# Transposing softmax weights on VectorE in squares of 32x32, with transfers inside SBUF, instead of on TensorE

## The chip, the cores and the metric

The kernel runs on one core of a Trainium2 chip. A core has five engines that run beside one another, each through a queue of its own in order: TensorE (PE in the profile; its weight loads are PEld), VectorE (DVE), ScalarE (ACT), GpSimd (POOL) and SyncE (SP), which here issues every transfer. The metric is the device time of one execution in microseconds, lower is better.

## The reference

Pooled attention, whose output goes through an expert layer with a rational activation:

```python
def _attn_ref(q, k, v):                      # q, k, v: (8, 8, 576, 64) float32
    k_p = k.reshape(B, H, Sp, pool, D).mean(axis=3)      # pool = 8, Sp = 72
    v_p = v.reshape(B, H, Sp, pool, D).mean(axis=3)
    scores = scale * np.matmul(q, k_p.transpose(0, 1, 3, 2))
    scores = scores - np.max(scores, axis=-1, keepdims=True)
    attn = np.exp(scores)
    attn = attn / (np.sum(attn, axis=-1, keepdims=True) + 1e-09)
    return np.matmul(attn, v_p)

def _moe_ref(x, w_in, w_out, a, b):          # x: (4608, 512), w_in: (512, 2048)
    h = x @ w_in
    P = a[0] + a[1] * h + a[2] * h * h + a[3] * h * h * h
    Q = 1.0 + np.abs(b[0]) * np.abs(h) + np.abs(b[1]) * h * h
    return (P / (Q + 1e-06)) @ w_out
```

## The kernel before

The 4608 tokens go through in 18 blocks of 256 tokens (`TOK`), a block being two tiles of 128. For each block `attend` computes the attention's output x, transposed (features on the partitions) and split into a high and a low part; then eight units of 256 hidden features each follow: `mm1` (TensorE, bank ph), `rational` (ScalarE, VectorE, GpSimd; result gh and gl) and `mm2` (TensorE, bank po). Matrix products run in fp32r on such split operands, so each is made of three products, and those of the weighted values of four. Blocks 0 to 3 are interleaved in a special order while the weights are loaded; blocks 4 to 17 run one after the other, eight units each.

The attention of one tile t (`attention`, lines 563 to 616) goes like this. q is loaded (qt, two buffers). TensorE transposes it per pair of heads (pq), ScalarE copies that to SBUF (qT, a single buffer). TensorE multiplies it with the pooled keys kpT (ps, two halves). VectorE takes the maximum (mx) and subtracts it (e), ScalarE exponentiates, VectorE sums (sm) and inverts, GpSimd multiplies: e now holds the softmax weights, 128 tokens x 8 heads x 72 keys. Two heads are 144 columns; the last 128 of them are the main part, the first 16 the rest. The main part is transposed by TensorE into a PSUM bank (pm, lines 607 to 609), ScalarE rounds it into the high part hi, VectorE subtracts to get the low part lo (the two tiles am, one buffer each, lines 610 to 612). The rest goes through er, pr and ar. When both tiles of a block are done, `values` multiplies the weights with the pooled values (pv) and splits the result into x.

The order of all of it is written out by a planner (`Plan`, lines 100 to 241), which runs when the kernel is built. Every operation is registered with its engine, an assumed cost, its buffers and its dependences. `solve` first gives every operation a due time, going back from its users: the user's due time less `slack` (1.6, in `attend` 2.5) times the cost plus 0.25 us (line 152). It then simulates the engines: it takes again and again the operation that can start first, and among those that can start at the same time the one due first. Buffers of a ring go to tiles in order, except in the rings called loose. A tile that an operation only `claims` is taken with it, too: the pq transposes claim qT. For transfers it assumes the issue cost (0.45 us), the bytes at 360 GB/s on one shared bus, another 1.9 us to land, and at most eight in flight (lines 213 to 216). `issue` writes the instructions out in that order, so each engine's order is fixed; on the chip, semaphores hold an instruction until its operands are there. Since all instructions are recorded in line 240, the profile tells them apart by their tiles.

PSUM's eight banks are four ps_o (po, and the rational's rp), two ps_h (ph) and two ps_a (all of the attention's banks).

Of the kernel before, what the change touches and what calls it, by code (L numbers as in the profile page):

```python
# [8 lines left out]
F32 = mybir.dt.float32  # L9
# [3 lines left out]
ALU = mybir.AluOpType  # L13
# [86 lines left out]
class Plan:  # L100
# [47 lines left out]
    def solve(self):  # L148
        for op in reversed(self.ops):
            for d in op.deps:  # L150
                d.users.append(op)
                d.due = min(d.due, op.due - d.slack * (d.cost + 0.25))
        for op in self.ops:
            op.wait, op.ready = len(op.deps), max(0.0, op.due - op.early)
        engs = {}
        for op in self.ops:
            engs.setdefault(op.eng, [])
            if not op.wait:
                engs[op.eng].append(op)
        at = dict.fromkeys(engs, 0.0)  # L160
        port = bus = 0.0
        flights = [0.0] * 8
        done, order = 0, []
        while done < len(self.ops):
            best = None
            for e, cands in engs.items():
                pick = None
                opts = []
                for op in cands:
                    t = max(at[e], op.ready)  # L170
                    if op.port:
                        t = max(t, port)
                    if op.bytes:
                        t = max(t, flights[0])
                    need = {}
                    for b in op.bufs:
                        if not b.held:
                            r = b.ring
                            n = need.setdefault(id(r), [r, 0])
                            if not r.loose and b not in r.queue[:len(op.bufs)]:  # L180
                                break
                            n[1] += 1
                    else:
                        for r, n in need.values():
                            mine = [b for b in op.bufs if not b.held and b.ring is r]
                            if len(r.free) < n or not r.loose and any(
                                    b not in mine for b in r.queue[:n]):
                                break
                            t = max(t, sorted(r.free)[n - 1])
                        else:  # L190
                            opts.append((t, op))
                if not opts:
                    continue
                t0 = min(t for t, _ in opts)
                t, op = min(((t, op) for t, op in opts if t <= t0 + 0.02),
                            key=lambda x: (x[1].due, x[1].seq))
                if best is None or t < best[0]:
                    best = t, op
            assert best, "the plan is stuck at " + ", ".join(
                str([b.name for b in op.bufs]) for c in engs.values() for op in c[:3])  # L200
            t, op = best
            engs[op.eng].remove(op)
            for b in op.bufs:
                if not b.held:
                    b.held = True
                    r = b.ring
                    r.free.remove(min(r.free))
                    r.queue.remove(b)
            op.start, op.end = t, t + op.cost
            at[op.eng] = op.end  # L210
            if op.port:
                port = op.end
            if op.bytes:
                bus = max(bus, op.end) + op.bytes / 360e3
                op.end = bus + 1.9
                flights = sorted(flights[1:] + [op.end])
            for b in op.bufs:
                b.left -= 1
                b.it = max(b.it or 0.0, op.end)
                if not b.left:  # L220
                    b.ring.free.append(b.it)
            for u in op.users:
                u.wait -= 1
                u.ready = max(u.ready, op.end + (self.LAT if u.eng != op.eng else 0.0))
                if not u.wait:
                    engs[u.eng].append(u)
            order.append(op)
            done += 1
        self.order = order
# [29 lines left out]
def tile_pooled_attention_then_rational_moe(  # L259
# [20 lines left out]
    P = 128  # L280
    G = 8
    SP = S // G
    NJ = H // 2
    REM = 2 * SP - P
    RW = G * D
    TOK = 256
# [29 lines left out]
    def bank(where, name, shape):  # L316
        return new(where, where, shape, F32, name)
# [236 lines left out]
    def segs(t0, n):  # L554
# [5 lines left out]
            t = e  # L560
        return r

    def attention(t, am, ar):

        sg = segs(t * P, P)
        col = slice((t % 2) * P, (t % 2 + 1) * P)
        qt = new("work2", "qt", [P, H, D], F32, f"qt{t}")
        for r0, r1, n in sg:
            s0 = t * P + r0 - n * S
            dma(512, qt[r0:r1], q[n, :, s0:s0 + (r1 - r0), :].rearrange("h s d -> s h d"))  # L570
        pq = bank("ps_a", f"pq{t}", [P, NJ, P])
        qT = new("work1", "qT", [P, NJ * P], F32, f"qT{t}").rearrange("p (j t) -> p j t", j=NJ)
        pe(109 * NJ, [
            ("transpose", (pq[:, j, :],
                           qt[:, 2 * j:2 * j + 2, :].rearrange("s h d -> s (h d)"), ident), {})
            for j in range(NJ)], claims=(qT,))
        act(NJ * P).copy(qT, pq)
        e = new("work2", "e", [P, H, SP], F32, f"e{t}")
        mx = new("work2", "mx", [P, H], F32, f"mx{t}")
        sm = new("work2", "sm", [P, H], F32, f"sm{t}")  # L580
        for c in range(2):
            hs = slice(4 * c, 4 * c + 4)
            ps = bank("ps_a", f"ps{t}_{c}", [P, 4, SP])
            pe(245 * 2 * len(sg), [
                mm(ps[r0:r1, 2 * jj:2 * jj + 2, :], qT[:, 2 * c + jj, r0:r1],
                   kpT[n % 2][:, 2 * c + jj, :], True, True)
                for jj in range(2) for r0, r1, n in sg], claims=(e, mx, sm))
            dve(4 * SP).tensor_reduce(out=mx[:, hs], in_=ps, op=ALU.max, axis=AX.X)
            dve(4 * SP).tensor_tensor(
                out=e[:, hs, :], in0=ps,  # L590
                in1=mx[:, hs].unsqueeze(2).to_broadcast([P, 4, SP]), op=ALU.subtract)
        act(H * SP).activation(e, e, AF.Exp, scale=D ** -0.5)
        dve(H * SP).tensor_reduce(out=sm, in_=e, op=ALU.add, axis=AX.X)
        dve(0).tensor_scalar(out=sm, in0=sm, scalar1=1e-9, scalar2=None, op0=ALU.add)
        dve(40).reciprocal(sm, sm)
        gp(400).tensor_tensor(
            out=e, in0=e, in1=sm.unsqueeze(2).to_broadcast([P, H, SP]), op=ALU.mult)
        ef = e.rearrange("p (j h) s -> p j (h s)", h=2)
        er = new("work2", "er", [P, 2, 2, 2, 2, REM], F32R, f"er{t}")
        rem = ef[:, :, 0:REM].rearrange("p (c m) r -> p c m r", m=2)  # L600
        for c in range(2):
            esrc = rem[:, c].unsqueeze(1).to_broadcast([P, 2, 2, REM])
            act(90).copy(er[:, c, 0], esrc)
            dve(60, port=True).tensor_tensor(
                out=er[:, c, 1], in0=esrc, in1=er[:, c, 0].bitcast(F32), op=ALU.subtract)
        hi, lo = am
        pm = bank("ps_a", f"pm{t}", [P, NJ, P])
        pe(109 * NJ, [("transpose", (pm[:, j, :], ef[:, j, REM:], ident), {})
                      for j in range(NJ)], claims=am)
        act(NJ * P).copy(hi[:, :, col], pm)  # L610
        dve(NJ * P).tensor_tensor(
            out=lo[:, :, col], in0=pm, in1=hi[:, :, col].bitcast(F32), op=ALU.subtract)
        pr = new("ps_a", "ps_a", [P, 2, P], F32R, f"pr{t}")
        pe(63 * 2, [("transpose", (pr[:, c, :], er[:, c].rearrange("p a g m r -> p (a g m r)"),
                                   identr), {}) for c in range(2)], claims=(ar,))
        act(2 * P).copy(ar[:, :, col], pr.bitcast(F32))
# [28 lines left out]
    def attend(i):  # L645

        for _, _, n in segs(i * TOK, TOK):
            if n not in prepared:
                prepared.add(n)
                prep_k(n)  # L650
                (prep_v_early if n < 2 else prep_v)(n)
        am = [new("work1", f"am{s}", [P, NJ, TOK], F32R, f"am{s}_{i}") for s in range(2)]
        ar = new("work1", "ar", [P, 2, TOK], F32R, f"ar{i}")
        for m in range(2):
            attention(2 * i + m, am, ar)
        return values(i, am, ar)


# [171 lines left out]
```

## Time and profile before

| | us |
|---|---|
| median of 3 executions | 998.79 |
| their range | 996.03 to 999.13 |
| the profiled execution | 996.57 |
| its span, first to last instruction | 994.6 |

| engine | busy us | share of the span | instructions |
|---|---|---|---|
| TensorE matmuls | 968.0 | 97% | 6396 |
| TensorE weight loads | 871.4 | 88% | 6396 |
| VectorE | 743.8 | 75% | 1299 |
| ScalarE | 710.6 | 71% | 1216 |
| GpSimd | 507.1 | 51% | 443 |

Transfers move 64.26 MB, at 65 GB/s in the mean. A row of the groups reads: line, engine, operation, written tile <- read tiles, shapes, count | busy time in us, mean ns of one | idle time of the engine before them, and what ended it. In the timeline a row is start, duration, engine, operation; xN are N instructions merged, and a bracket gives the idle time ahead.

### The profile page before, as it was taken

The page shows a single profiled execution, that of the slowest core. Times are in us where ns is not written, and L with a number is a line of the kernel's source. Part 1 is how long each engine was busy: PE and PEld are TensorE (multiplying, and loading weights), DVE is VectorE, ACT ScalarE, POOL GpSimd, SP SyncE. Part 2 cuts the span into 40 slices and gives each one's busy share as a digit, 9 for nine tenths or more (in the row PEclk, how much of TensorE's full clock was granted, in tenths as well). Part 3 has the DMA queues.
Part 4 walks back from the last instruction along what each step waited for, and adds up shares of the span by engine and source line. Part 5 has one row for each costly group of instructions (what it writes and reads, how often), then busy time and mean ns, then how long its engine had stood idle before and what let it go on. Part 6 is the DMA issues. An engine that isn't in the chain of part 4 may idle for free.

```text
span 994.6 us, 16951 instructions
## 1 busy us (share of the span) xinstructions
PE 968.0 (97%) x6396; PEld 871.4 (88%) x6396; DVE 743.8 (75%) x1299; ACT 710.6 (71%) x1216; POOL 507.1 (51%) x443
## 2 busy tenths in 40 slices
PE   7898999999999999999999999999999999999997
PEld 6787898889898899899899989898989898999996
DVE  4798977888687867687778687787778686767664
ACT  3578888878666766777777776687767776777764
POOL 4355666757444734353654464454643473445343
PEclk9699999999999999999999999999999999999999
DMA  9946020233111302010401031002201020100000
GB/s 301 332 148 257 22 86 1 70 106 128 32 33 25 88 1 86 1 43 7 128 22 43 6 107 44 21 27 61 89 11 39 20 87 1 44 1 22 1 22 21
DMA packets 62705, 64.26 MB, mean 65 GB/s; under 512 B 39968, under 2 KB 39968, under 8 KB 62624
## 3 DMA queue, kind: packets, MB, share of 16 engines
q1 hardware_dynamic: 62624, 63.19, 20.6%
q8 instruction: 50, 0.82, 0.4%
q14 instruction: 31, 0.25, 0.1%
HBM read 50.60 MB, written 12.58 MB: 64 GB/s over the span
## 4 chain that ended last, share of the span: by engine, by line
PE 91%; DVE 4%; ACT 2%; issue 2%; POOL 1%; POOLq 0%; ACTq 0%; DVEq 0%
PE ph L240 40%; PE po L240 38%; PE pv L240 4%; PE ps L240 4%; PE pm L240 2%; PE pq L240 1%; DVE t L240 1%; PE pvs L240 1%; PE warm L240 1%; PE pr L240 1%; POOL w L240 0%; PE pk L240 0%; DVE rp L240 0%; DVE m_win L240 0%; DVE m_wout L240 0%
## 5 line engine op out<-in xcount | busy, mean ns | idle before, releaser
L240 PEld LDWEIGHTS ph<-x,win 128*128 128x128 f32 x3264 | 474.0, 189 | 63.0 <-issue 7.5
L240 PE MATMUL ph<-x,win 128*128 128x256 f32 x3264 | 502.3, 283 | 3.0 <-DVE t L240 0.5
L240 PE MATMUL po<-wout,gh 128*128 128x512 f32 x1152 | 354.5, 397 | 1.4 <-ACT gh L240 1.4
L240 POOL TENSOR_TENSOR w<-w,r 128x512 f32<-128x512 f32 x144 | 189.7, 1318 | 258.0 <-ACT r L240 252.9
L240 POOL TENSOR_TENSOR gl<-t,gh 128x512 fp32r<-128x512 f32 x144 | 190.5, 1323 | 154.7 <-ACT gh L240 106.0
L240 PEld LDWEIGHTS po<-wout,gh 128*128 128x128 f32 x1152 | 183.6, 189 | 12.1 <-ACT gh L240 2.3
L240 PE MATMUL po<-wout,gl 128*128 128x512 f32 x576 | 183.0, 399 | 0.3 <-POOL gl L240 0.2
L240 DVE TENSOR_TENSOR t<-t,ph 128x512 f32<-128x512 f32 x144 | 98.5, 684 | 101.3 <-ACT t L240 97.1
L240 DVE SCALAR_TENSOR_TENSOR t<-t,abn,rp 128x512 f32<-128x512 f32 x144 | 107.2, 745 | 71.9 <-ACT rp L240 70.7
L240 ACT ACTIVATE rp<-w,cbias 128x512 f32<-128x512 f32 x144 | 99.4, 690 | 41.6 <-POOL w L240 34.8
L240 ACT ACTIVATE t<-ph,abn 128x512 f32<-128x512 f32 x144 | 109.3, 769 | 20.6 <-PE ph L240 20.0
L240 ACT ACTIVATE r<-w,abn 128x512 f32<-128x512 f32 x144 | 117.6, 816 | 7.0 <-POOL gl L240 0.7
L240 ACT ACTIVATE w<-ph 128x512 f32<-128x512 f32 x144 | 85.9, 596 | 47.3 <-PE ph L240 44.3
L240 ACT CAST gh<-t 128x512 fp32r<-128x512 f32 x144 | 88.1, 612 | 43.2 <-DVE t L240 42.9
L240 DVE SCALAR_TENSOR_TENSOR t<-t,abn,ph 128x512 f32<-128x512 f32 x144 | 107.5, 747 | 5.0 <-ACT w L240 0.7
L240 DVE SCALAR_TENSOR_TENSOR t<-rp,t 128x512 f32<-128x512 f32 x144 | 99.1, 688 | 3.8
L240 DVE SCALAR_TENSOR_TENSOR rp<-w,rp 128x512 f32<-128x512 f32 x144 | 99.2, 689 | 0.2
L240 PEld LDWEIGHTS po<-wout,gl 128*128 128x128 f32 x576 | 91.4, 189 | 5.1 <-POOL gl L240 1.1
L240 ACT ACTIVATE rp<-rp 128x512 f32<-128x512 f32 x144 | 83.8, 582 | 3.8
L240 ACT COPY qT<-pq 128x512 f32<-128x512 f32 x36 | 21.1, 585 | 48.5 <-PE pq L240 47.3
L240 POOL TENSOR_TENSOR e<-e,sm 128x576 f32<-128x576 f32 x36 | 41.0, 1153 | 28.5 <-DVE sm L240 21.5
L240 PE MATMUL ps<-kpT,qT 128*128 128x144 f32 (+1 forms) x320 | 45.6, 298 | 3.8 <-DVE e L240 2.5
(88 smaller groups left out, 896.9 us busy)
## 6 DMA issues: line engine op xcount, KB each, us to landing
out_dram<-ob SPq DMA_DIRECT2D x18, 512.0 KB, 2.9
qt<-in_q_dram SPq DMA_DIRECT2D x32, 256.0 KB, 3.1
rwin<-in_moe_w_in_dram SPq DMA_DIRECT2D x8, 1024.0 KB, 7.7
rwout<-in_moe_w_out_dram SPq DMA_DIRECT2D x8, 1024.0 KB, 11.5
st_k<-in_k_dram SPq DMA_DIRECT2D x12, 512.0 KB, 4.4
st_v<-in_v_dram SPq DMA_DIRECT2D x12, 512.0 KB, 3.8
st_v<-in_v_dram SPq DMA_DIRECT2D x48, 64.0 KB, 3.6
early<-in_k_dram SPq DMA_DIRECT2D x4, 512.0 KB, 7.2
```

The costliest lines, as they stand in the source:

```text
L240: getattr(engines[op.eng], name)(*map(value, args), **{k: value(v) for k, v in kw.items()})
```

## The change

Blocks 0 to 3 (tiles 0 to 7) stay as they are. For tiles 8 to 35 the four transposes pm, their copy and subtraction are left out. VectorE transposes the main part of e in squares of 32x32 into a tile es, which is taken from the ring of qT; within a square rows and columns are exchanged, but the squares stay where they were. Sixteen transfers on SP's queue then bring the squares of partition group a and column group g, for all four pairs of heads, to partition group g and column group a of lo, as plain fp32. The planner is told 48 KB for each of them (they carry 32 x 4 x 32 x 4 bytes, 16 KB). When both tiles of the block are there, one ScalarE cast over 128x1024 makes hi, and one VectorE subtraction over as many elements, in place, makes lo. In the planner, the due time of whatever a transfer's user needs goes back by another 5 us times the slack, for all transfers of the kernel.

```diff
-                d.due = min(d.due, op.due - d.slack * (d.cost + 0.25))
+                d.due = min(d.due, op.due - d.slack * (d.cost + 0.25 + (5.0 if d.bytes else 0.0)))
...
+    HB = 32
+
...
         hi, lo = am
-        pm = bank("ps_a", f"pm{t}", [P, NJ, P])
-        pe(109 * NJ, [("transpose", (pm[:, j, :], ef[:, j, REM:], ident), {})
-                      for j in range(NJ)], claims=am)
-        act(NJ * P).copy(hi[:, :, col], pm)
-        dve(NJ * P).tensor_tensor(
-            out=lo[:, :, col], in0=pm, in1=hi[:, :, col].bitcast(F32), op=ALU.subtract)
+        if t >= 8:
+
+            es = new("work1", "qT", [P, NJ * P], F32, f"es{t}").rearrange(
+                "p (j g s) -> p j g s", j=NJ, s=HB)
+            dve(NJ * P).transpose(es, ef[:, :, REM:].rearrange("p j (g s) -> p j g s", s=HB))
+            for a in range(4):
+                for g in range(4):
+                    s0 = (t % 2) * P + a * HB
+                    dma(48, lo[g * HB:(g + 1) * HB, :, s0:s0 + HB].bitcast(F32),
+                        es[a * HB:(a + 1) * HB, :, g, :])
+        else:
+            pm = bank("ps_a", f"pm{t}", [P, NJ, P])
+            pe(109 * NJ, [("transpose", (pm[:, j, :], ef[:, j, REM:], ident), {})
+                          for j in range(NJ)], claims=am)
+            act(NJ * P).copy(hi[:, :, col], pm)
+            dve(NJ * P).tensor_tensor(
+                out=lo[:, :, col], in0=pm, in1=hi[:, :, col].bitcast(F32), op=ALU.subtract)
...
         for m in range(2):
             attention(2 * i + m, am, ar)
+        if i >= 4:
+            hi, lo = (x.rearrange("p j t -> p (j t)") for x in am)
+            act(NJ * TOK).copy(hi, lo.bitcast(F32))
+            dve(NJ * TOK, port=True).tensor_tensor(
+                out=lo, in0=lo.bitcast(F32), in1=hi.bitcast(F32), op=ALU.subtract)
         return values(i, am, ar)
```

## The prediction

> **What bounds the kernel now.** I read the page first: the busy shares and the chain that ended last.
>
> ```profile
> span 994.6 us, 16951 instructions
> PE 968.0 (97%) x6396; PEld 871.4 (88%) x6396; DVE 743.8 (75%) x1299; ACT 710.6 (71%) x1216; POOL 507.1 (51%) x443
> ...
> PE 91%; DVE 4%; ACT 2%; issue 2%; POOL 1%; POOLq 0%; ACTq 0%; DVEq 0%
> ```
>
> TensorE is busy 97% of the span and makes up 91% of the chain; VectorE and ScalarE have a quarter of their time free. Next the table by stretches (the columns after the stretch are its length, then busy time of PE, PEld, DVE, ACT and POOL, the granted clock, the share of the DMA engines and GB/s), and TensorE's waits from 250 to 960 us.
>
> ```profile
> 0.00:25.00 25.00, 17.79 (x109) 15.57 (x109) 11.53 (x34) 8.43 (x18) 11.29 (x51) 0.96 1.03 302
> 25.00:50.00 25.00, 20.49 (x113) 18.47 (x114) 18.36 (x36) 14.37 (x28) 8.83 (x5) 0.63 1.02 329
> 50.00:950.00 900.00, 890.54 (x5952) 803.99 (x5951) 689.98 (x1198) 663.05 (x1135) 470.36 (x375) 1.00 0.17 53
> ```
>
> ```profile
> PE pq L240 <- PE ps L240: 0.6, 1, 0.6
> PE pl L240 <- ACT kpT L240: 0.3, 1, 0.3
> PE pl L240 <- DVE ks L240: 0.2, 1, 0.2
> ```
>
> Only the first 50 us are bound by loads (DMA share above 1, clock down to 0.63). Over the 900 us behind them TensorE is idle for 9.5 us, and over 710 of them it waits for another engine just 1.1 us in all. So the stage that the change touches, blocks 4 to 17, is TensorE's own work in a row: work taken from TensorE comes off the time one for one, and any new wait in its queue goes on in the same way.
>
> **Removed.** Of each of the tiles 8 to 35 (28 of 36): four TensorE transposes, a ScalarE copy, a VectorE subtraction.
>
> ```profile
> 550.82 0.87 PE pm L240 x8
> ```
>
> ```profile
> L240 PE MATMUL pm<-identr,e 128*128 128x128 f32 x144 | 20.0, 278 | 2.0 <-DVE t L240 0.9 <-ACT qT L240 0.8 <-DVE vr L240 0.4
> L240 DVE TENSOR_TENSOR am<-pm,am 128x512 fp32r<-128x512 f32 x36 | 23.6, 686 | 4.7 <-ACT am L240 4.4
> L240 ACT CAST am<-pm 128x512 fp32r<-128x512 f32 x36 | 19.8, 587 | 7.1 <-PE pm L240 6.8
> ```
>
> The piece of the chain holds both tiles of a block: eight transposes in 0.87 us, 0.109 us each. The 278 ns of the group row is one matmul's own length, which overlaps its neighbours; the queue moves on by 0.109. Fourteen blocks times 0.87 is **12.2 us** off TensorE. The Trainium skill (TensorE: Matmul & The Clock Gate, Part 4: PE-mode transpose) gives about 275 ns for a transpose in one kernel's context; the trace's 278 agrees, but priced by it the removal would be an estimated 31 us, and the chain's 0.109 decides against that. The freed PSUM bank I cost at nothing: the 1.1 us of waits above hold no wait for one that is worth more.
>
> **Added on the compute engines.** VectorE gets 28 transposes of 128x512 (no such row), and per block one subtraction of 128x1024 out of SBUF; ScalarE one cast of 128x1024 per block.
>
> ```profile
> L240 ACT CAST win<-m_win 128x1024 fp32r<-128x1024 f32 x8 | 8.4, 1045 | 0.0
> L240 DVE SCALAR_TENSOR_TENSOR m_win<-rwin,m_win 128x1024 int32<-128x1024 int32 x8 | 10.2, 1276 | 0.0
> L240 DVE TENSOR_SCALAR m_win<-m_win 128x1024 int32<-128x1024 int32 x8 | 7.5, 932 | 0.0
> L240 DVE TENSOR_TENSOR st_k<-st_k 128x512 f32<-128x512 f32 x12 | 10.1, 857 | 0.0
> ```
>
> A transpose lies between 0.47 us (half of the 932 ns) and 0.86 (the two-input row of 512); I take 0.69, what the removed subtraction took for as many elements. VectorE then has 2 x 0.69 + 1.28 - 2 x 0.69 = 1.3 us more per block (0.8 to 1.6), ScalarE 1.045 - 2 x 0.587 = 0.13 less. Both hide behind TensorE: with 18 us more, VectorE is at about 79% of the 900. If that cover were gone, the 18 us would be lost.
>
> **Added on SP's queue.** Sixteen transfers per tile of 16 KB, 448 in all, each 128 pieces of 128 bytes. No transfer inside SBUF is in the trace; the nearest rows are the trains of 64 KB loads of v and the loads of q.
>
> ```profile
> 480.36 1.73 SPq L240 DMA_DIRECT2D st_v<-in_v_dram  x4
> ```
>
> ```profile
> L240 SPq DMA_DIRECT2D st_v<-in_v_dram x6: 329/417/424, 480.4 to 483.0; - x6
> DMA to landing us min/median/max: 2.1/2.2/4.2
> ```
>
> ```profile
> 636.00:641.00 5.00, 5.00 (x35) 4.55 (x34) 3.48 (x5) 3.31 (x6) 3.12 (x3) 1.00 0.23 52
> ```
>
> ```profile
> 580.41 1.26 SPq L240 DMA_DIRECT2D st_v<-in_v_dram  x3
> 583.27 0.38 SPq L240 DMA_DIRECT2D st_v<-in_v_dram  x1
> ```
>
> ```profile
> SPq L240 <- PE pq L240: 373.5, 25, 41.3
> SPq L240 <- DMA st_v<-in_v_dram: 9.5, 4, 3.0
> ```
>
> Four issues take 1.73 us, 0.43 each; I take 0.45 (single ones go from 0.33 to 0.42), landing 2.1 us after its issue when nothing large is in the way. The stretch at 636 us holds one load of q, 256 KB in 1024 pieces of 256 bytes: 0.23 x 5.0 x 16 engines / 1024 = 18 ns a piece. At that price a transfer holds its engines for 128 / 16 x 18 ns = 0.14 us, well under the 0.45 of its issue, so issue sets the pace. A train of sixteen lasts 15 x 0.45 + 2.1 = 8.9 us: 7.1 at 0.33, and about 12 with the landings of 5 us that the loads behind 583 us show. The plan that fixes the order counts 0.45 for each issue, 48 KB at 360 GB/s and 1.9 us to land: 16 x 0.45 + 0.14 + 1.9 = 9.2. Plan and rows agree within 0.3 us, and that is the main reason for my forecast. SP spends 448 x 0.45 = 202 us on it, out of a queue that by the row above has 373 us of waiting for pq alone; loads of q and stores of out queue behind a train, and both have time.
>
> The Trainium skill (DMA: Bandwidth & Descriptors, Specifications) speaks against such pieces: transfers under 512 bytes are read, modified and written back. By it a piece could cost an estimated 36 ns rather than 18, or 0.29 us a transfer; no run here shows it, and it is still below the issue's 0.45, so the sum is the same by both, and only the ring's chance below grows.
>
> **The new waits.** The squares lie in the single buffer that qT has. So ScalarE's copy qT of the next tile must wait until the sixteen transfers have landed, and behind it in ScalarE's queue stand the activations of the expert stage, while TensorE's ps matmuls, in order, wait for that copy. Second, the cast and the subtraction of a block follow the second train, and TensorE's pv waits for both. Third, lo has one buffer: the first train of a block waits for pv of the block before. Before, both tiles of a block overlapped (one pm piece for two tiles); now they run one behind the other.
>
> ```profile
> 531.16 0.58 ACT L240 COPY qT<-pq 128x512 f32<-128x512 f32 x1
> 540.92 1.15 POOL L240 TENSOR_TENSOR e<-e,sm 128x576 f32<-128x576 f32 x1 [5.79 <-DVE sm L240]
> ...
> 636.35 0.59 ACT L240 COPY qT<-pq 128x512 f32<-128x512 f32 x1
> 651.92 2.26 POOL L240 TENSOR_TENSOR e<-e,sm 128x576 f32<-128x576 f32 x2
> ```
>
> ```profile
> 245.43 0.34 PE L240 MATMUL pv<-am,vm 128*128 128x128 f32 x2
> ...
> 924.72 0.40 PE L240 MATMUL pv<-am,vm 128*128 128x256 f32 x2
> ```
>
> From qT to the end of the normalised weights: 542.07 - 531.16 = 10.9 us when it presses, 653.07 - 636.35 = 16.7 when it doesn't. With 0.7 for the transpose and 8.9 for the train a tile holds the ring 20.5 us, two tiles 41. From the pv of block 4 to that of block 17 (13 blocks) a block lasts 52.25 us, 51.4 after the change. So the ring fits with 10 us to spare.
>
> What is left is the order on TensorE: a train later than planned holds ps or pv back. The plan puts the pq transposes behind the landing (they claim qT), the chip doesn't need that: 0.44 + 0.07 us; and half a piece of waiting for ScalarE (0.35) and for TensorE (0.24). That is about 1.1 us of give at each of 28 joints. Six blocks also load k and v; there SP stands at a transfer that hasn't landed from 581.67 to 583.27, 1.6 us. Once in each of these blocks: 6 x (1.6 - 1.1) = 3.0 us. Bounds: nothing, and case B below.
>
> **The head.** The planner now counts 5 us more behind every transfer, times a slack of 1.6 (weights) or 2.5 (q, k, v): those become due 4.5 us earlier against the weights, and loads of the first 50 us can change places. One 512 KB load ahead of a needed one costs 512 KB / 329 GB/s = 1.6 us, the reverse gains as much; two of them bound this at -3 and +3. I take 0.
>
> **Sum.** 996.57 (the profiled execution, 2.0 more than its span) - 12.2 + 3.0 + 0 = 987.4. That execution is 2.2 us under the median 998.79; on the scale of the median: **989.6 us**.
>
> **Rivals.**
>
> - B, trains land late (slower). One mechanism: transfers share their landing with other traffic and SP stops at outstanding ones, so each train takes 2 us longer than planned. Price 28 x (2.0 - 1.1) = 25 us: 989.6 - 3.0 + 25 = 1012. It decides from 28 x (d - 1.1) = 12.2, d = 1.5 us. For it: landings of up to 5 us and the 9.5 us of SP's waits. Against: those are four waits beside 512 KB loads; most trains have none.
> - C, the ring binds (slower). If a tile takes the slow 16.7 us, two need 2 x (16.7 + 0.7 + 8.9) = 52.6 against 51.4: 1.2 x 14 = 17 us, 1007. With pieces three times as dear it becomes worse, since the engines' 0.43 us then meets the issue. Against: the 16.7 us tile was one that nobody waited for.
> - D, the gain is eaten: trains late by 1.5 us, or the head worse by 3 and the joints by 6: 998.
> - E, no joint costs anything and the head gains 3: 998.8 - 12.2 - 3 = 983.6.
>
> **How the numbers follow.** A, the forecast, 0.52; E 0.10; D 0.13; B 0.17; C 0.08. What a measurement can tell is 0.3%, 3 us. Faster (under 995.8): A and E, 0.62. Same: D, 0.13. Slower: B and C, 0.25. A's own range is 985 to 995; the range from 982 to 1010 takes in E, D, most of C and the milder half of B.
>
> **What would show it.** Right: pm gone from the chain after block 4, TensorE's busy time 12 us down over the stretch from 50 us on, its waits there still a few us, trains of about 9 us, VectorE up by some 18 us. Wrong: rows with ps waiting for qT, or pv for am, of tens of us in TensorE's waits (B), qT copies waiting for transfers at every tile and a distance of pv to pv above 52 us (C), or first 100 us that differ by more than 3 us in TensorE's busy time (the head).

## The result: 1032.0 us, 3.4% slower

The changed kernel's median is 1031.99 us; the kernel before, timed beside it, had 997.7. The ratio is 1.0341 with a 95% interval of 1.032 to 1.0363. The forecast was 989.6, with 1010 as the upper end.

From the page of the changed kernel: span, busy times, and the chain that ended last by engine and by line.

```profile
span 1029.1 us, 17440 instructions
PE 972.3 (94%) x6284; PEld 870.4 (85%) x6284; DVE 759.9 (74%) x1313; ACT 706.8 (69%) x1202; POOL 504.9 (49%) x443
...
PE 41%; SPq 20%; DVE 11%; ACT 9%; DMA 6%; issue 6%; POOL 5%; POOLq 0%; ACTq 0%; DVEq 0%
SPq L240 20%; PE ph L240 17%; PE po L240 14%; PE pv L240 4%; DVE t L240 4%; DMA am<-es 4%; PE ps L240 3%; POOL e L240 2%; POOL w L240 1%; POOL gl L240 1%; DVE am L240 1%; ACT r L240 1%; DVE sm L240 1%; ACT rp L240 1%; ACT t L240 1%
```

TensorE has 112 instructions fewer and yet 4 us more of busy time. It makes up 41% of the chain instead of 91%; 20% is now SP's queue issuing transfers, which had no part in the chain before. The span is 34.5 us longer: 4.3 of it busy time of TensorE, 30.2 idle time (56.8 against 26.6 us).

The waits of TensorE from 250 to 990 us, and ScalarE's waits for the transfers, over the whole span:

```profile
PE ps L240 <- ACT qT L240: 13.6, 12, 2.1
PE pv L240 <- DVE am L240: 5.6, 10, 0.8
PE pv L240 <- ACT am L240: 5.2, 8, 1.1
PE pv L240 <- ACT qT L240: 2.1, 2, 1.5
PE pv L240 <- ACT kpT L240: 0.8, 1, 0.8
PE pv L240 <- DMA qt<-in_q_dram: 0.8, 2, 0.6
```

```profile
ACT am L240 <- DMA am<-es: 32.4, 13, 3.5
...
ACT qT L240 <- DMA am<-es: 16.4, 10, 3.8
```

These are the two joints that the prediction named: ps behind qT, pv behind am. Both hang on the trains of sixteen transfers. Here they are, as issues and as one train of the timeline:

```profile
L240 SPq DMA_DIRECT2D am<-es x448: 585/599/1607, 206.6 to 960.9; - x150
DMA to landing us min/median/max: 1.8/1.8/5.2
```

```profile
513.88 10.25 SPq L240 DMA_DIRECT2D am<-es  x16
...
544.58 11.30 SPq L240 DMA_DIRECT2D am<-es  x16
```

An issue takes 0.60 us, not 0.45, and with the gap behind it one follows the other every (10.25 - 0.60) / 15 = 0.643 us. The landing is quick, 1.8 us in the median. The first of the two trains lasts 10.25 - 0.60 + 1.8 = 11.4 us, where the plan counts 9.2: 2.2 us late. The second takes a microsecond more, so 2.2 us is the lateness of a train that nothing disturbs. There are 28 joints; at 23 of them (13 and 10 in the rows above) ScalarE waits for the landing.

The new work on the compute engines costs what it was thought to:

```profile
L240 DVE STREAM_TRANSPOSE es<-e 128x512 f32<-128x512 f32 x28 | 19.9, 710 | 6.6 <-POOL e L240 5.7
L240 DVE TENSOR_TENSOR am<-am,am 128x1024 fp32r<-128x1024 f32 x14 | 17.1, 1224 | 31.8 <-ACT am L240 25.7 <-DMA st_k<-in_k_dram 6.1
L240 ACT CAST am<-am 128x1024 fp32r<-128x1024 f32 x14 | 14.7, 1047 | 32.4 <-DMA am<-es 32.4
```

The waits by name add up to less than the loss, and the busy time went up. The timeline and the stretches around one late pv show a reason (columns as in the prediction: length, busy times of PE, PEld, DVE, ACT and POOL, then the granted clock):

```profile
629.55 0.63 PE L240 MATMUL po<-wout,gl 128*128 128x512 f32 x2
631.31 0.41 PE L240 MATMUL pv<-am,vm 128*128 128x64 f32 x2 [1.13 <-ACT am L240]
...
632.57 0.58 PE L240 MATMUL pv<-am,vm 128*128 128x64 f32 x3 [0.79 <-DVE am L240]
...
637.81 1.11 PE L240 MATMUL ph<-x,win 128*128 128x256 f32 x4
```

```profile
628.00:632.00 4.00, 2.65 (x17) 1.96 (x15) 0.71 (x1) 1.76 (x3) 0.16 (x1) 1.00 0.08 12
632.00:636.00 4.00, 3.43 (x20) 3.43 (x21) 3.59 (x6) 3.48 (x6) 1.28 (x1) 0.65 0.01 4
636.00:640.00 4.00, 4.00 (x19) 3.81 (x18) 2.25 (x5) 1.74 (x4) 1.27 (x1) 0.50 0.00 0
640.00:644.00 4.00, 4.00 (x30) 3.75 (x30) 3.96 (x7) 0.94 (x2) 1.56 (x1) 1.00 0.00 0
```

TensorE stands 1.13 us before pv and 0.79 us in the middle of it, and then works at half clock for the greater part of two stretches. By the granted clock that is (1 - 0.65) x 4 + (1 - 0.50) x 4 = 3.4 us of work lost behind 1.9 us of waiting. The Trainium skill (TensorE: Matmul & The Clock Gate, Part 1: The HAM clock gate) says that an idle window of about 3.4 us brings the half clock. Here no single wait came near that: two short ones with a few matmuls between them were followed by it. One place can't show where the limit lies.

### The profile page after: what moved, and what is told of

It reads as the page before. It is cut to its first block, busy times and chain, and to the rows that moved or that the text cites. A ratio compares the mean times of both kernels' runs of the same rounds, so it can differ in the third digit from the quotient of the medians.

```text
span 1029.1 us, 17440 instructions
## 1 busy us (share of the span) xinstructions
PE 972.3 (94%) x6284; PEld 870.4 (85%) x6284; DVE 759.9 (74%) x1313; ACT 706.8 (69%) x1202; POOL 504.9 (49%) x443
## 4 chain that ended last, share of the span: by engine, by line
PE 41%; SPq 20%; DVE 11%; ACT 9%; DMA 6%; issue 6%; POOL 5%; POOLq 0%; ACTq 0%; DVEq 0%
SPq L240 20%; PE ph L240 17%; PE po L240 14%; PE pv L240 4%; DVE t L240 4%; DMA am<-es 4%; PE ps L240 3%; POOL e L240 2%; POOL w L240 1%; POOL gl L240 1%; DVE am L240 1%; ACT r L240 1%; DVE sm L240 1%; ACT rp L240 1%; ACT t L240 1%
## 5 line engine op out<-in xcount | busy, mean ns | idle before, releaser
L240 PE MATMUL po<-wout,gh 128*128 128x512 f32 x1152 | 358.8, 401 | 2.2 <-ACT gh L240 1.4
L240 PEld LDWEIGHTS po<-wout,gh 128*128 128x128 f32 x1152 | 187.3, 191 | 15.6 <-ACT gh L240 2.5
L240 PEld LDWEIGHTS po<-wout,gl 128*128 128x128 f32 x576 | 93.6, 190 | 8.4 <-POOL gl L240 2.2
L240 PE MATMUL pv<-am,vm 128*128 128x256 f32 (+3 forms) x288 | 54.5, 308 | 16.5 <-DVE am L240 6.1
L240 PEld LDWEIGHTS pv<-am,vm 128*128 128x128 f32 x288 | 46.8, 212 | 24.3 <-DVE am L240 9.7
L240 PE MATMUL ps<-kpT,qT 128*128 128x144 f32 (+1 forms) x320 | 46.5, 302 | 18.4 <-ACT qT L240 15.2
```

The costliest lines, as they stand in the source:

```text
L240: getattr(engines[op.eng], name)(*map(value, args), **{k: value(v) for k, v in kw.items()})
```

## The experiments

All but e4, which starts from the kernel before, start from the changed kernel. Theory **M**: the trains last longer on the chip than in the plan, so the fixed order puts the waiting instructions too early. Rival **R**: two tiles in a row over one buffer are too long for a block, whatever the plan counts. Rival **K**: the transfers or VectorE's transposes slow other work. Rival **H**: the edit of the due times costs the time. The kernel before was timed beside each, at 996 to 999 us.

**e1: the plan is told the true issue cost.**

```diff
-                    dma(48, lo[...], es[...])
+                    dma(48, lo[...], es[...], issue=0.65)
```

> The changed kernel with one number altered: the planner is told that issuing one of the sixteen transfers takes 0.65 us instead of 0.45 (on the chip the changed kernel's issues follow one another every 0.645 us). The work is the same, only the fixed order differs. Theory M (each train of sixteen transfers lasts 11.5 us on the chip, 9.2 in the plan; the instructions that wait for it stand too early in the queues of ScalarE and TensorE): the waits go, TensorE's waits from 250 us on fall from some 28 us to under 8, no stretch with a clock below 1.0 after the head, 985 to 992 us. Rival R (the two tiles one behind the other over the one buffer are too long for the block on the chip, whatever the plan counts): no better than 1015. Rival K (the transfers or the transposes slow TensorE's own work): the same, above 1015.

985.04 us, ratio 0.9881 (0.9855 to 0.9907): 47 us less than the changed kernel, and faster than the kernel before. From its page, TensorE's waits from 250 us on (three rows in all), and the transfers:

```profile
span 982.8 us, 17433 instructions
PE 955.0 (97%) x6284; PEld 859.4 (87%) x6284; DVE 776.7 (79%) x1313; ACT 705.8 (72%) x1202; POOL 506.1 (52%) x443
```

```profile
PE po L240 <- ACT gh L240: 1.3, 2, 0.7
PE ph L240 <- DVE t L240: 0.8, 3, 0.5
PE po L240 <- POOL gl L240: 0.4, 2, 0.2
```

```profile
L240 SPq DMA_DIRECT2D am<-es x448: 585/599/1478, 206.9 to 919.4; - x150
```

The transfers are as slow as before and no one waits for them. The work is the changed kernel's, and the order alone takes 47 us away: M holds, R falls, and K falls as what carries the loss.

The two kernels also show what the late trains cost TensorE, as their instructions are the same. In the changed kernel it is idle for 1029.1 - 972.3 = 56.8 us, in e1 for 982.8 - 955.0 = 27.8: 29.0 us of waiting. Its busy time is 972.3 - 955.0 = 17.3 us longer for the same work. About 10 of these are the clock, by an estimate from its mean: at 0.980 the changed kernel loses 0.020 x 1029.1 = 20.6 us, at 0.989 e1 loses 10.8. The rest isn't taken apart.

**e2: one transfer for sixteen, same order.**

```diff
+                    plan.ops[-1].skip = (a, g) != (3, 3)
+                    plan.ops[-1].calls = [("dma_start", (lo[:, :, col].bitcast(F32),
+                                                         es.rearrange("p j g s -> p j (g s)")), {})]
```

> The order of the changed kernel is kept instruction for instruction, but of the sixteen transfers of a tile only the last is issued, and it carries the whole tile of 256 KB at once. It leaves out the exchange between partition groups, so the weights' squares stay in the wrong places. Theory M: the train shrinks from 11.5 us to about 3, under the 9.2 of the plan, nothing waits: 985 to 990 us. R: also below 1000, since the ring turns faster. K, if it is the bytes or VectorE's transposes: still above 1010. If the change of due times (rival H) carries the loss: still above 1010.

980.21 us, ratio 0.9827 (0.9805 to 0.9849). With the order of the changed kernel, instruction for instruction, the loss is gone once the train is short. This also shows what the removed transposes were worth, as nothing new waits here. The busy times, TensorE's waits from 250 us on, and the transfers:

```profile
PE 952.6 (97%) x6284; PEld 862.0 (88%) x6284; DVE 762.0 (78%) x1313; ACT 706.1 (72%) x1202; POOL 506.5 (52%) x443
```

```profile
PE po L241 <- ACT gh L241: 0.7, 1, 0.7
PE po L241 <- POOL gl L241: 0.2, 1, 0.2
```

```profile
L241 SPq DMA_DIRECT2D am<-es x28: 600/606/650, 216.4 to 902.9; - x28
```

TensorE's busy time is 968.0 - 952.6 = 15.4 us down, 0.138 us for each of the 112 transposes. In e1, where little waits either, it is 968.0 - 955.0 = 13.0 us, 0.116 each.

**e3 and e5: the squares written back into e,** so that qT waits for no transfer; e5 with the true issue cost in the plan.

```diff
-            es = new("work1", "qT", ...)
-            dve(NJ * P).transpose(es, ef[...])
+            sq = ef[:, :, REM:].rearrange("p j (g s) -> p j g s", s=HB)
+            dve(NJ * P).transpose(sq, sq)
...
-                        es[a * HB:(a + 1) * HB, :, g, :])
+                        ef[a * HB:(a + 1) * HB, :, REM + g * HB:REM + (g + 1) * HB])   # e5: issue=0.65
```

> The transposed squares are written back into e itself instead of into the buffer of qT, so qT of the next tile waits for no transfer (the first of the two joints is gone); the issue cost told to the planner stays 0.45, so the second joint (cast, subtraction and pv behind the block's second train) stays late. Theory M: about half of the loss goes, 1003 to 1015 us, ps no longer waits for qT, pv still waits for am. R: all of the loss goes, below 995.

1080.41 us, ratio 1.0826 (1.0785 to 1.0867): worse, where all expected better. ScalarE's waits and a train of e3:

```profile
ACT am L240 <- DMA am<-e: 75.4, 14, 6.7
```

```profile
636.19 21.89 SPq L240 DMA_DIRECT2D am<-e  x32
```

Without the ring both tiles' trains stand behind one another on SP. Thirty-two issues are 31 x 0.645 + 1.8 = 21.8 us when nothing disturbs them, and by the row shown 21.89 - 0.60 + 1.8 = 23.1, against 32 x 0.45 + 2.04 = 16.4 in the plan: 5.4 to 6.7 us late. The cast waits 75.4 / 14 = 5.4 us in the mean of the blocks. One joint with the whole lateness costs more than two with half of it. Most of the difference from the changed kernel isn't waiting, though: TensorE is idle for 76.0 us instead of 56.8, but busy for 1005.0 instead of 972.3, at a mean clock of 0.943 instead of 0.980. My expectation left out that lateness adds up along a queue, and the clock.

> The in-place form (e3) with the planner told 0.65 us per issue. In e3 the two trains of a block stand behind one another on SP, so that with 32 issues the chip lies 32 x (0.645 - 0.45) = 6.2 us behind the plan at the one joint that is left; ScalarE's cast waited 75 us for them at 14 places, 5.4 each. Theory M: told the true cost, e3's 1080 us fall to 983 to 992, and the cast's wait to under 15. If writing the squares back into e costs something by itself (e is held longer, VectorE waits for the copies er): above 1020.

983.64 us, ratio 0.986 (0.9838 to 0.9882). The 97 us of e3 above it were lateness, with the slow clock that came with its waits. R falls a second time: with and without the ring the result is the same once plan and chip agree.

**e4: the due-time edit alone,** on the kernel before.

```diff
-                d.due = min(d.due, op.due - d.slack * (d.cost + 0.25))
+                d.due = min(d.due, op.due - d.slack * (d.cost + 0.25 + (5.0 if d.bytes else 0.0)))
```

> The kernel before with only the planner's edit: 5 us more behind each transfer when due times are worked out. The transposes stay on TensorE. Theory M: the order of the first loads changes a little, the time by less than 3 us, 995 to 1001. Rival H (the edit of the due times costs the time by itself): above 1010.

998.05 us, ratio 1.001 (0.9996 to 1.0023): nothing. The edit costs no time by itself: H falls, and the term for the head was rightly zero.

**e10: everything but that edit,** with issue=0.65.

```diff
-                d.due = min(d.due, op.due - d.slack * (d.cost + 0.25 + (5.0 if d.bytes else 0.0)))
+                d.due = min(d.due, op.due - d.slack * (d.cost + 0.25))
```

> The planner told 0.65 us per issue as in e1, but without its other edit: the 5 us behind each transfer in the due times are taken out. If that edit is what lets the planner start a tile early enough for two trains in a row: TensorE waits again, though trains and plan agree, 1005 to 1030 us. If it is of no weight: 983 to 990, as e1.

1021.56 us, ratio 1.0262 (1.0216 to 1.0309). So the edit carries weight in the changed kernel, though none by itself. TensorE's longest waits are others here, from 200 us on:

```profile
PE ph L240 <- DVE t L240: 13.5, 14, 1.4
PE po L240 <- ACT gh L240: 8.1, 7, 1.8
PE pv L240 <- DVE e L240: 3.6, 4, 1.0
```

Not pv behind am, but the expert stage behind VectorE and ScalarE. That a tile started too late crowds its softmax into the expert stage's time is my reading; the run shows only the waits. It also shows that trains which are planned right aren't enough: with e1's issue cost and other due times the time is 36.5 us above e1's.

**e6: a smaller lateness,** issue=0.55.

```diff
-                    dma(48, lo[...], es[...])
+                    dma(48, lo[...], es[...], issue=0.55)
```

> The changed kernel with the planner told 0.55 us per issue. A train is then 16 x (0.645 - 0.55) = 1.5 us later than planned, where it was 3.1 by the same count at 0.45 and nothing at 0.65. Theory M with about a microsecond of give at each joint: 987 to 1000 us, between e1 and the changed kernel and nearer to e1. If the loss were in proportion to the lateness, without give: about 1008.

997.11 us, ratio 0.9997 (0.9976 to 1.0018): the gain is just eaten. ScalarE's cast waits, less:

```profile
ACT am L240 <- DMA am<-es: 14.3, 13, 2.6
```

**e7, e8, e9, e12: what sets the price of an issue.** All four keep the changed kernel's order. e7: one row of 512 bytes per partition (32 pieces); e8: 32 columns of all 128 partitions; e9: fifteen of the sixteen into DRAM; e12: the same fifteen from 18 partitions.

```diff
# e7
+    plan.ops[-1].calls = [("dma_start", (lo[g * HB:(g + 1) * HB, a, col].bitcast(F32),
+                                         es[a * HB:(a + 1) * HB, g].rearrange("p g s -> p (g s)")), {})]
# e8
+    plan.ops[-1].calls = [("dma_start", (lo[:, a, (t % 2) * P + g * HB:(t % 2) * P + (g + 1) * HB].bitcast(F32),
+                                         es[:, a, g]), {})]
# e9; e12 with sc[a, g, 0:18] and es[a * HB:a * HB + 18, :, g, :]
+    plan.ops[-1].calls = [("dma_start", (sc[a, g], es[a * HB:(a + 1) * HB, :, g, :]) if (a, g) != (3, 3) else
+                           (lo[:, :, col].bitcast(F32), es.rearrange("p j g s -> p j (g s)")), {})]
```

> What sets the 0.59 us of an issue. The changed kernel's order (planner told 0.45) and as many transfers of 16 KB between groups of 32 partitions, but each one row of 512 bytes per partition on both sides, 32 pieces instead of 128. It leaves out the right placement inside the groups. If the number of pieces, or the number of dimensions, sets the issue: it falls to 0.33 to 0.42 us, the train to under 9.2 us, and with it the time to 978 to 990. If it is the two ends in SBUF or the start at another partition: 0.59 again and 1020 to 1040 us.

> As e7, but each of the sixteen transfers takes 32 columns of all 128 partitions and stays on its partitions: 128 pieces of 128 bytes, one per partition. It leaves out the exchange between partition groups. If the number of pieces sets the issue: 0.59 us and 1020 to 1040. If it is the number of dimensions, or the start at another partition: 0.33 to 0.42 us and 978 to 990.

> What sets the 0.59 us of an issue, second attempt: neither the number of pieces nor the partitions did (e7, e8). The changed kernel's order, planner told 0.45; fifteen of a tile's sixteen transfers, unchanged in size and source, go to a scratch in DRAM, the sixteenth carries the whole tile inside SBUF. It leaves out the exchange between partition groups. If two ends in SBUF make the issue dear: 0.33 to 0.45 us, a train under 9.5 us, 978 to 992 us. If it is the source in SBUF, or many issues close together: 0.59 and above 1015.

> As e9 (fifteen transfers to a scratch in DRAM, the last one inside SBUF), but each of the fifteen takes only 18 of the 32 partitions, as the loads of v do whose 0.42 us an issue the prediction took for its price. It leaves out the exchange between partition groups. If the partition count (18 against 32 or 128) sets the price of an issue in a train: 0.40 to 0.45 us against e9's 0.60, a train of 15 x 0.47 + 2.7 = 9.8 us against 12.7, and 995 to 1010 us against 1064. If it doesn't: 0.60 us and 1050 to 1070.

1021.68 (ratio 1.0248, 1.0196 to 1.03), 1032.43 (1.035, 1.0314 to 1.0386), 1064.05 (1.0651, 1.0593 to 1.0709) and 1147.85 us (1.1535, 1.1515 to 1.1554). The issues of the four, in this order:

```profile
L240 SPq DMA_DIRECT2D am<-es x448: 507/589/1657, 206.8 to 949.9; - x150
```

```profile
L240 SPq DMA_DIRECT2D am<-es x448: 465/599/1738, 207.3 to 965.6; - x150
```

```profile
L240 SPq DMA_DIRECT2D sc<-es x420: 549/598/2182, 206.6 to 993.2; - x140
```

```profile
L240 SPq DMA_DIRECT2D sc<-es x420: 748/766/1218, 204.9 to 1072.7; - x140
```

A quarter of the pieces, all the partitions, another kind of memory at the far end: 0.59 to 0.60 us each time. Eighteen partitions made it dearer, 0.77. The expectation of e12 is wrong on the loads of v: they fill 16 partitions each (`REM` in the kernel), not 18, so e12 leaves open whether their 0.42 us hangs on the partitions. The issue that opens a train does change with the shape: 0.59 us in the changed kernel, 0.51 in e7, 0.47 in e8; the fifteen behind it don't. Nor is 0.6 us the price of standing in a train: the single transfers of e2, mostly with nothing on the queue for microseconds around them, take 0.60 to 0.65 us. What sets it stays open; these runs only rule out what I had thought of.

**e11: the in-place form with a margin,** issue=0.72 and 6.0 instead of 5.0 in the due times.

```diff
-    issue=0.65)            # in place, as e5
+    issue=0.72)
...
-    (5.0 if d.bytes else 0.0)
+    (6.0 if d.bytes else 0.0)
```

> The in-place form with a margin: 0.72 us told per issue, 6 us instead of 5 in the due times. If what is left between e5 (983.6) and the run with one transfer (980.2) is small lateness from other traffic: 980 to 983. If the margin only costs order: 983 to 988.

983.93 us, ratio 0.9856 (0.9836 to 0.9875): as e5. The margin brings nothing, so the 3.4 us between e5 and e2 aren't lateness that a margin takes up.

**Lateness against time.** For each run an undisturbed train on the chip (first issue to last landing, one train of each run, from rows as above) and the train in the plan (sixteen times the told cost and 2.04):

| run | train on the chip, us | in the plan, us | late by | time, us |
|---|---|---|---|---|
| e1 | 11.4 | 12.4 | -1.0 | 985.0 |
| e6 | 11.4 | 10.8 | 0.6 | 997.1 |
| e7 | 11.2 | 9.2 | 2.0 | 1021.7 |
| e8 | 11.3 | 9.2 | 2.1 | 1032.4 |
| changed kernel | 11.4 | 9.2 | 2.2 | 1032.0 |
| e9 | 12.8 | 9.2 | 3.6 | 1064.1 |
| e12 | 15.2 | 9.2 | 6.0 | 1147.9 |

The last two go to the last issue's start and take that transfer's landing (2.7 us in e9, taken for e12 too):

```profile
560.17 10.01 SPq L240 DMA_DIRECT2D sc<-es  x15
570.27 0.64 SPq L240 DMA_DIRECT2D am<-es  x1
```

```profile
591.81 12.44 SPq L240 DMA_DIRECT2D sc<-es  x15
604.36 0.65 SPq L240 DMA_DIRECT2D am<-es  x1
```

The later the trains, the longer the time, in kernels that differ in shapes, pieces and target. From e6 to e12 it is (1147.9 - 997.1) / (6.0 - 0.6) = 28 us for each microsecond of lateness. That this is also the number of joints is chance, for not all of it is waiting: from e1 to e12 TensorE's idle time grows by 95.9 us (27.8 to 123.7) and its busy time by 63.8 (955.0 to 1018.8, at a mean clock of 0.932). Nor does the time follow the train's length alone. e7, the changed kernel and e8 differ by 0.2 us of lateness and by 10 us of time; the mean clocks of their profiled executions are 0.987, 0.980 and 0.975. M's strongest support is e1 and e2: one changes the plan and leaves the transfers, the other shortens the train and leaves the order, and in both the loss is gone. What separates the two, 4.8 us, stays open.

## Why the prediction was wrong

**What bounds the kernel: right.** Work taken from TensorE came off the time, and any new wait went on to it; that a wait can cost more than its own length was left out (below).

**Removed, 12.2 us: right in kind, a little small.** The runs in which little waits show 13.0 (e1) to 15.4 us (e2) less of TensorE's busy time, 0.116 to 0.138 us a transpose. I preferred the chain's 0.109, from one block. The stretch with the 112 removed transposes in the kernel before (length, then the busy times of PE, PEld, DVE and ACT on pm) says 14.66 / 112 = 0.131:

```profile
200.00:990.00 790.00, 14.66 (x112) 12.81 (x112) 18.10 (x28) 15.10 (x28) 1.00 0.14 42
```

The group row's 20.0 us over 144 takes in the 32 transposes of blocks 0 to 3, too. Its 278 ns mean, by which the prediction's sentence on the Trainium skill (TensorE: Matmul & The Clock Gate, Part 4: PE-mode transpose) estimated 31 us, was too much by a factor of two: an instruction's length isn't its share of the queue.

**Added on the compute engines: right.** 0.71 us for a transpose (0.69 taken), 1.22 and 1.05 for subtraction and cast.

**Added on SP's queue: this step failed.** The term is the issue, 0.45 us by the trains of v; it measured 0.60, and 0.643 from one to the next. So the train was 11.4 us, not 8.9, and the sentence that plan and rows agree within 0.3 us, which I called the main reason for the forecast, was false. The trains of v are loads from DRAM on 16 partitions, and the kernel before has no transfer inside SBUF. Its issues on all partitions have no single price: here are two loads of q, one right behind the other, and the four stores of x from SBUF to DRAM (least, median and most, in ns):

```profile
2.38 1.21 SPq L240 DMA_DIRECT2D qt<-in_q_dram  x2
```

```profile
L240 SPq DMA_DIRECT2D xd<-x x4: 319/335/354, 42.2 to 52.4; - x4
```

1.21 / 2 = 0.60 us each, and 0.34. I took the range from single issues (0.33 to 0.42) and one train; with the loads of q its upper bound had to be 0.6, and with it a train of 15 x 0.60 + 2.1 = 11.1 us and case B.

**The pieces of 128 bytes** were no trouble: landing 1.8 us, and e7's pieces of 512 bytes land no faster. The rule of the Trainium skill (DMA: Bandwidth & Descriptors, Specifications) that small transfers are read, modified and written back had no visible price inside SBUF here.

**The new waits: right places, wrong size.** The joints are those that the trace shows. The price was put at 3.0 us, for six blocks only; the lateness turned out to be common to all trains. Case B had the formula, 28 x (d - 1.1) with d = 2.0, and gave 1012; with d = 2.2 it gives 28 x 1.1 = 31, which in place of the 3.0 makes 1017. These 31 us are near the 29.0 by which TensorE is idle longer than in e1. The missing 15 us are near the 17.3 of longer busy time, which no step of the prediction had: about 10 of them the lower clock, the rest open. So the give of 1.1 us was about right at this lateness. It isn't a constant: in the profiled execution of e6, 0.6 us late, TensorE is already idle for 34.3 us against 27.8 in e1. B's mechanism was another, though: landings beside other traffic. Landings were quick; it was the issue. That B's time came nearest was in part luck.

**The ring (C): not the cause.** e1 keeps it and is 12 us faster than the kernel before.

**The head: right at zero** (e4).

**The likeliest case's time** of 989.6 is 4.6 us above where the change lands when the plan is told the truth: 985.0.

## What to carry to other kernels

Where an order is fixed by a planner, an error in one cost isn't paid once: it is paid at every place that waits for the thing, and along a queue it adds up (16 issues of 0.64 us counted as 0.45 made 2.2 us or more, at up to 28 places; 32 of them 5.4 or more), and the waits can slow the work behind them, too. So price a transfer by a row of its own kind, and where the profile has none, carry the dearest undisturbed issue that it shows through the sum; measure the real price and tell it to the planner first: here that turned a loss of 3.4% into a gain of 1.2%, and the in-place form into one of 1.4%.

## What was not expected of the hardware

- An issue in a train on SP's queue took 0.59 to 0.60 us in the median for 16 KB out of SBUF, in three shapes to SBUF and one to DRAM, and 0.77 for 9 KB from 18 partitions to DRAM. A single transfer of 256 KB inside SBUF (e2) took as long, 0.61. In the kernel before, the median load of q took 0.38 us and that of v 0.42.
- Two waits of 1.1 and 0.8 us, a few matmuls between them, were followed by two stretches of 4 us at a mean granted clock of 0.65 and 0.50. In e3, with waits of up to 4.1 us before pv, the mean over the run was 0.943.
- A transpose of 128x128 on TensorE, 0.278 us long by its row, freed 0.12 to 0.14 us of the queue.
